# Queries, keys and the next input rows: loads moved to the GpSimd queue

## The chip, the core and the metric

The kernel runs on one NeuronCore of a Trainium2 chip. The metric is the device time of one launch in microseconds (us), taken as a median over runs. A profiled execution of the same program gives the trace from which every duration below is read.

## What is computed

Two independent heads are computed and their outputs laid side by side. Head A is a long convolution done through Fourier transforms. Head B is a recurrent attention over 64 segments of 32 rows, each preceded by 8 memory rows that the segment before has produced:

```python
for s in range(n_seg):
    xs = x[:, s * seg_len:(s + 1) * seg_len, :].copy()
    h = jnp.concatenate([mem, xs], axis=1)
    q = jnp.einsum('btd,dhe->bhte', h, Wq)
    k = jnp.einsum('btd,dhe->bhte', h, Wk)
    v = jnp.einsum('btd,dhe->bhte', h, Wv)
    scores = jnp.einsum('bhqe,bhke->bhqk', q, k) * scale
    scores = jnp.where(mask[None, None], scores, -1000000000.0)
    p = _softmax(scores, axis=-1)
    o = jnp.einsum('bhqk,bhke->bhqe', p, v)
    o = jnp.einsum('bhte,hed->btd', o, Wo)
    mem = o[:, :M, :].copy()
    outs.append(o[:, M:, :])
```

There are 32 heads of 128, a model width of 1024, and a segment needs the memory rows of the one before, so segments cannot run side by side.

## The kernel before

A first phase, some 390 us long, does head A and, beside it, the projections of the last 8 rows of every segment, which do not depend on the memory. Their queries and keys go to a DRAM tensor `QKBd` and their values to `VBd`.

Then comes the loop over the 64 segments (L948); one pass is called a turn here. A turn treats the 32 rows that are 8 memory rows and the segment's first 24. Heads are worked on in four groups of eight (`u0` to `u3`): `qk_part` (L787) multiplies the transposed rows `hT` with the group's query and key weights, `v_part` (L803) with the value weights of two groups, `tr_a` (L825) transposes, `scores` (L848) forms the masked scores, `softmax` (L870) turns them into probabilities `P`, `blocks` (L887) spreads these into `PB`, `pv` (L896) multiplies with the values, and `wo` (L911) with the output weights, all groups summing into one accumulator `Y`. `Y` is copied to `Y_sb`, its memory rows are transposed by `fill_mem` (L932) into the next `hT` at L936, and the next turn begins.

Not all weights fit on the chip. A turn streams 17 pairs of 512 KB from DRAM through a ring of 5 buffers (`wring`). `done` (L768) calls `place` (L686) when TensorE has used a pair, and `place` issues the next load on SyncE's queue at L691. The loads keep one fixed order: query and key pairs, value pairs, output pairs, as the turn uses them; in two places of a turn a ring buffer is filled from a copy parked in PSUM (L762, L763) instead.

Besides the ring a turn moves five small things. `load_h` (L701) fetches the next turn's input rows into the tile `H` (128 partitions of 512 bytes, 64 KB), on ScalarE's queue at L708; `h_rows` (L923) transposes `H` on TensorE at L927, between `pv(u3)` and `wo(u3)`. `load_b` (L834) fetches the segment's own queries and keys from `QKBd` into `qkb` (512 pieces of 256 bytes, 128 KB), on SyncE's queue at L836; the next turn reads it first in `tr_a(u0)` (a GpSimd copy, L830). GpSimd's queue itself issues the old rows' accumulator `OLd` (L909, 64 KB), four output stores (L1030, 12 KB each) and the values `VB` (`load_vb`, L846, 64 KB). `qkb` and `H` have one buffer each; `H` shares its buffer with the tile `qks` of L800.

The order of every queue is the order in which the program is written (`manual_schedule`, L43). So the place of a call in the loop decides what stands before and behind it on its engine. Each group's `softmax` begins with a GpSimd instruction that clears half of `P` (L873); `P` has one buffer, so the clearing waits until `blocks` of the group before has read it.

Before the loop, L943 and L944 call `load_vb(0)` and `load_b(0)`, in that order.

Of the kernel before, what the change touches and what calls it, by code (L numbers as in the profile page):

```python
# [21 lines left out]
def fused_kernel(ctx: ExitStack, tc, q, k, v, shift_k, ssm_k, ssm_D, outa, x, mem0, Wq, Wk, Wv, Wo, outb, n_seg):  # L22
# [11 lines left out]
    nc = tc.nc  # L34
    S, D = 2048, 1024
    NP = 34
# [14 lines left out]
    QKBd = dram.tile([4, 128, n_seg * 128], BF, name="QKBd")  # L51
# [61 lines left out]
    def res_half(key, n):  # L113
        if key not in res:
            if key in early:
                res[key] = wide["t"][:, early.index(key)]
            else:
                res[key] = res_pool[key].tile([128, 2, 1024], BF, name=f"W{key[0]}{key[1]}_{key[2]}")
        nc.sync.dma_start(res[key][:, n, :], half_src(key, n))
        return res[key][:, n, :]  # L120
# [580 lines left out]
    def load_h(s):  # L701

        H_ = acte.tile([128, 256], BF, tag="qks", name="H")
        if s == 0:
            nc.gpsimd.dma_start(H_[0:32, :], mem0.rearrange("t (dq c) -> (t dq) c", dq=4))
            nc.gpsimd.dma_start(H_[32:128, :], x[0:24].rearrange("t (dq c) -> (t dq) c", dq=4))
        else:
            nc.scalar.dma_start(H_[:], x[32 * s - 8:32 * s + 24].rearrange("t (dq c) -> (t dq) c", dq=4))  # L708
        return H_

    H = load_h(0)
# [47 lines left out]
    def unpark():  # L759
        while to_copy:  # L760
            key, t = to_copy.pop(0)
            nc.scalar.copy(t[:, 0, :], park[key][0][:])  # L762
            nc.vector.tensor_copy(t[:, 1, :], park[key][1][:])  # L763
# [23 lines left out]
    def qk_part(u, kcs):  # L787
        if kcs[0] == 0:
            u.qk = ps_a.tile([128, 512], F32, tag="a", name="qkacc")
        for kc in kcs:  # L790
            w = pair(("qk", u.g, kc))
            for t in range(2):
                for c2 in range(2):
                    p0 = 32 * (2 * t + c2)
                    nc.tensor.matmul(u.qk[p0:p0 + 32, :], lhsT=hT[:, kc, :], rhs=w[:, t, c2 * 512:(c2 + 1) * 512],  # L795
                                     start=(kc == 0), stop=(kc == 7), tile_position=(0, p0))
            done(("qk", u.g, kc))

    def qk_out(u):
        u.qks = acte.tile([128, 512], BF, tag="qks", name="qks")  # L800
        nc.scalar.copy(u.qks[:], u.qk[:])  # L801
# [31 lines left out]

    def load_b(s):  # L834
        qkb = acte.tile([128, 4, 128], BF, tag="qkb", name="qkb")
        nc.sync.dma_start(qkb[:], QKBd[:, :, s * 128:(s + 1) * 128].rearrange("g e x -> e g x"))  # L836
        return qkb

    def new_u(g):
        u = G()  # L840
        u.g = g
        u.qkb = qkb[:, g, :]
        return u
# [4 lines left out]
    def scores(u):  # L848
        S = ps_ts.tile([128, 4, 40], F32, tag="ts", name="S")
        qb = u.qkb.rearrange("e (h t r) -> e h t r", h=8, t=2)  # L850
        for c in range(4):
            nc.tensor.matmul(S[32 * c:32 * c + 32].rearrange("p a k -> p (a k)"), lhsT=ident[:, 32 * c:32 * c + 32],
                             rhs=mask[:].unsqueeze(2).to_broadcast([128, 2, 2, 40]), start=True, stop=False,
                             tile_position=(0, 32 * c))
        for i in range(2):
            for c in range(4):
                hh = 2 * c + i
                nc.tensor.matmul(S[32 * c:32 * c + 32, i, :], lhsT=u.QT[:, hh, :], rhs=u.KT[:, hh, :],
                                 start=False, stop=False, tile_position=(0, 32 * c))
        for i in range(2):  # L860
            for c in range(4):
                hh = 2 * c + i
                nc.tensor.matmul(S[32 * c:32 * c + 8, 2 + i, :], lhsT=qb[:, hh, 0, :], rhs=u.KT[:, hh, :],  # L863
                                 start=False, stop=(i == 1), tile_position=(0, 32 * c))
        mx = act.tile([128, 4], F32, tag="mx", name="mx")
        nc.vector.tensor_reduce(out=mx[:], in_=S[:], op=ALU.max, axis=AX.X)  # L866
        nc.vector.tensor_tensor(out=S[:], in0=S[:], in1=mx[:].unsqueeze(2).to_broadcast([128, 4, 40]), op=ALU.subtract)  # L867
        return S

    def softmax(u, S):  # L870
        P = act.tile([128, 2, 2, 2, 32], BF, tag="P", name="P")
        k0 = 8 * u.g
        nc.gpsimd.memset(P[:, 1], 0.0)  # L873
        Sv = S[:].rearrange("p (a i) k -> p i a k", a=2)
        nc.scalar.activation(P[:, 0], Sv[:, :, :, 0:32], ACT.Exp, scale=scale)  # L875
        nc.scalar.activation(P[:, 1, :, :, k0:k0 + 8], Sv[:, :, :, 32:40], ACT.Exp, scale=scale)  # L876
        sm = act.tile([128, 4], F32, tag="sm", name="sm")
        Pv = P[:].rearrange("p b i a k -> p b (i a) k")
        nc.vector.tensor_reduce(out=sm[:], in_=Pv.rearrange("p b x k -> p x b k"), op=ALU.add, axis=AX.XY)  # L879
        nc.vector.reciprocal(sm[:], sm[:])  # L880
        nc.vector.tensor_tensor(out=Pv, in0=Pv, in1=sm[:].unsqueeze(1).unsqueeze(3).to_broadcast([128, 2, 4, 32]),  # L881
                                op=ALU.mult)
        Pf = P[:].rearrange("p b i a k -> p (b i a k)")
        nc.vector.transpose(out=Pf, in_=Pf)
        u.PT = P[:].rearrange("p b i a q -> p (b i) (a q)")
# [58 lines left out]
    qkb = load_b(0)  # L944
# [3 lines left out]
    for s in range(n_seg):  # L948
        last = s + 1 == n_seg
        def first_loads(g):  # L950
            for key in (n_o[g - 1:g] if s == 0 and g else ()):
                for n in range(2):
                    res_half(key, n)

        first_loads(0)
        us = [new_u(g) for g in range(4)]
        u0, u1, u2, u3 = us
        qk_part(u0, range(0, 5))
        unpark()
        qk_part(u0, range(5, 8))  # L960
        qk_out(u0)
        v_part(0, range(0, 4))
        tr_a(u0)
        unpark()
        first_loads(1)
        qk_part(u1, range(0, 4))
        S = scores(u0)
        softmax(u0, S)
        if s == 0:
            nc.vector.memset(PB[:], 0.0)  # L970
        blocks(u0, "DDDD")
        qk_part(u1, range(4, 8))
        qk_out(u1)
        v_part(0, range(4, 8))
        tr_a(u1)
        u0.v = u1.v = v_out()
        first_loads(2)
        qk_part(u2, range(0, 4))
        S = scores(u1)
        softmax(u1, S)  # L980
        if last:
            spare = [key for key in resident if key[0] != "o" and key[1] < 1 + (key[0] == "qk") and key not in early]
            for key, at in zip([key for key in streamed if key[0] == "o"], spare):
                nc.sync.dma_start(res[at][:], Wst[key])
                res[key] = res[at]
            for s0, s1 in ((0, 32), (32, s)):
                nc.sync.dma_start(OLs[:, s0:s1].rearrange("e s h r -> e (s h r)"),
                                  OLd[:, s0:s1].rearrange("e s x -> e (s x)"))
        qk_part(u2, range(4, 8))
        qk_out(u2)  # L990
        pv(u0, s)
        blocks(u1, "DDDD")
        first_loads(3)
        qk_part(u3, range(0, 2))
        tr_a(u2)
        qk_part(u3, range(2, 6))
        S = scores(u2)
        softmax(u2, S)
        qk_part(u3, range(6, 8))
        qk_out(u3)  # L1000
        v_part(1, range(0, 1))
        pv(u1, s)
        blocks(u2, "DDDD")
        v_part(1, range(1, 2))
        tr_a(u3)
        v_part(1, range(2, 5))
        S = scores(u3)
        if not last:
            H = load_h(s + 1)
            qkb = load_b(s + 1)  # L1010
        softmax(u3, S)
        v_part(1, range(5, 8))
        u2.v = u3.v = v_out()
        Y = ps_a.tile([128, 512], F32, tag="a", name="yacc")
        wo(u0, Y)
        pv(u2, s)
        blocks(u3, "DDAA")
        wo(u1, Y)
        wo(u2, Y)
        pv(u3, s)  # L1020
        if not last:
            hT = new_hT()
            h_rows(H, hT, 8)
        wo(u3, Y)
        Y_sb = act.tile([128, 256], BF, tag="P", name="Y_sb")
        nc.scalar.copy(Y_sb[:], Y[:, 0:256])  # L1026
        if not last:
            fill_mem(hT, Y_sb)
        for dq in range(4):
            nc.gpsimd.dma_start(outb[32 * s:32 * s + 24, dq * 256:(dq + 1) * 256], Y_sb[32 * dq + 8:32 * dq + 32, :])  # L1030
        if not last:
            load_vb(s + 1)
# [88 lines left out]
```

## Time and profile before

| | |
|---|---|
| median of 3 runs | 2093.33 us (2092.27 to 2094.11) |
| the profiled execution | 2093.32 us |
| its span, first to last instruction | 2091.5 us |
| mean granted TensorE clock | 0.984 |
| TensorE busy | 1702.4 us, 81% |
| VectorE busy | 1115.3 us, 53% |
| ScalarE busy | 908.7 us, 43% |
| GpSimd busy | 413.1 us, 20% |
| moved by DMA | 728.64 MB, 348 GB/s |

The span is cut into the first phase (to about 388 us), the loop (to about 2018 us) and a last stage that multiplies the kept rows with the output weights. A queue that issues DMAs is named with a q behind its engine (SPq, ACTq); GpSimd's issues are listed as busy time of POOL. A DMA queue of its own belongs to each issuing engine: q1 is fed by SyncE, q10 by ScalarE, q0 by GpSimd. "To landing" runs from the start of the issue to the semaphore that tells of the arrival.

### The profile page before, as it was taken

How to read it: one execution, taken by the hardware profiler on the slowest of the kernel's cores; microseconds unless marked ns; L12 is line 12 of the kernel's file. 1: busy time of each engine (PE TensorE's matmuls, PEld its weight loads, DVE VectorE, ACT ScalarE, POOL GpSimd, SP SyncE). 2: the span in 40 equal slices, each digit the busy share in tenths (PEclk: the TensorE clock that was granted, in tenths of full speed). 3: DMA queues.
4: the chain of work that ended last, by engine and by line, in shares of the span. 5: the costliest groups of instructions: out<-in, count | busy, mean ns of one | idle time of the engine just before them, and what ended most of it. 6: DMA issues, size and time to landing. Idle time of an engine off the chain costs nothing. (4 is left out here: it accounts for less than half of the span.)

```text
span 2091.5 us, 73911 instructions
## 1 busy us (share of the span) xinstructions
PE 1702.4 (81%) x30484; PEld 894.2 (43%) x30514; DVE 1115.3 (53%) x3313; ACT 908.7 (43%) x2276; POOL 413.1 (20%) x1018
## 2 busy tenths in 40 slices
PE   5888987888788888888887878888888878888879
PEld 2433233444444444444444444444444444444449
DVE  6986833355555555555555555555555555555541
ACT  5556731244444444444444444444444444444430
POOL 2004730121111111111111111111212121111110
PEclk9999999999999999999999999999999999999999
DMA  6899989999999999999999999999999999999980
GB/s 236 282 346 362 343 287 381 352 377 372 356 375 368 365 360 370 372 366 375 358 368 353 367 358 372 359 377 358 371 358 378 363 352 351 374 370 379 368 337 23
DMA packets 266384, 728.64 MB, mean 348 GB/s; under 512 B 65007, under 2 KB 77183, under 8 KB 265277
## 3 DMA queue, kind: packets, MB, share of 16 engines
q1 hardware_dynamic: 239486, 686.65, 88.8%
q0 software_dynamic: 15520, 22.06, 3.3%
q10 hardware_dynamic: 11040, 15.21, 2.1%
q8 instruction: 239, 3.92, 0.7%
q14 instruction: 99, 0.81, 0.1%
HBM read 673.52 MB, written 56.56 MB: 349 GB/s over the span
## 5 line engine op out<-in xcount | busy, mean ns | idle before, releaser
L795 PE MATMUL qkacc<-Wqk,hT 128*32 128x512 bf16 x4096 | 338.5, 383 | 0.0
L795 PEld LDWEIGHTS <-hT 128*32 128x32 bf16 x8192 | 184.9, 96 | 236.3 <-issue 84.2
L916 PEld LDWEIGHTS <-OT 128*32 128x32 bf16 x8192 | 210.1, 96 | 109.5 <-issue 59.2
L795 PE MATMUL qkacc<-wring,hT 128*32 128x512 bf16 x2048 | 204.9, 389 | 31.3 <-DMA wring<-Wstqk 25.5
L763 DVE COPY wring<-park 128x1024 bf16<-128x1024 bf16 x128 | 88.6, 692 | 239.4 <-PE vacc L809 124.8
L875 ACT ACTIVATE P<-S 128x128 bf16<-128x128 f32 x256 | 71.1, 278 | 330.4 <-DVE S L867 244.3
L809 PE MATMUL vacc<-Wv,hT 128*32 128x512 bf16 x2560 | 209.8, 382 | 0.0
L809 PE MATMUL vacc<-wring,hT 128*32 128x512 bf16 x1536 | 154.7, 387 | 65.5 <-DMA wring<-in_B_Wv_dram 63.6
L809 PEld LDWEIGHTS <-hT 128*32 128x32 bf16 x4096 | 113.0, 95 | 184.4 <-issue 108.3
L762 ACT COPY wring<-park 128x1024 bf16<-128x1024 bf16 x128 | 130.7, 1021 | 138.9 <-PE qkacc L795 112.8
L894 DVE COPY PB<-P 32x160 bf16<-32x160 bf16 x896 | 172.9, 193 | 10.6
L879 DVE TENSOR_REDUCE sm<-P 128x4 f32<-128x256 bf16 x256 | 107.5, 420 | 128.6 <-ACT P L876 128.6
L831 ACT COPY QK<-tp 128x256 bf16<-128x256 bf16 x256 | 95.4, 373 | 185.7 <-PE tp L822 184.5
L795 PE MATMUL qkacc<-Wearly,hT 128*32 128x512 bf16 x2048 | 161.0, 391 | 18.4 <-DVE hT L936 17.9
L830 POOL COPY QK<-qkb 128x64 bf16<-128x64 bf16 x256 | 61.3, 239 | 564.5 <-PE tp L822 404.8
L916 PE MATMUL yacc<-wring,OT 128*32 128x256 bf16 x2520 | 126.7, 274 | 37.4 <-DMA wring<-Wsto 35.2
L905 ACT CAST OT<-otacc 128x256 bf16<-128x256 f32 x256 | 98.7, 386 | 130.4 <-PE otacc L901 130.4
L801 ACT CAST qks<-qkacc 128x512 bf16<-128x512 f32 x256 | 151.1, 590 | 4.2 <-PE qkacc L795 3.5
L1030 POOL DMA_DIRECT2D out_dram<-Y_sb x256 | 129.1, 511 | 84.8 <-ACT Y_sb L1026 82.8
L822 PE MATMUL tp<-ident,qks 128*128 128x128 bf16 x1024 | 102.4, 223 | 52.6 <-ACT qks L801 50.3
L866 DVE TENSOR_REDUCE mx<-S 128x4 f32<-128x160 f32 x256 | 83.2, 325 | 85.2 <-PE S L863 79.5
L901 PE MATMUL otacc<-PB,vsb 128*128 128x160 bf16 x512 | 97.6, 238 | 35.3 <-ACT vsb L816 35.3
(212 smaller groups left out, 2957.1 us busy)
## 6 DMA issues: line engine op xcount, KB each, us to landing
wring<-Wstqk SPq DMA_DIRECT2D x448, 512.0 KB, 6.2
wring<-in_B_Wv_dram SPq DMA_DIRECT2D x320, 512.0 KB, 6.7
wring<-Wsto SPq DMA_DIRECT2D x315, 512.0 KB, 6.3
SK<-s_sb SPq DMA_DIRECT2D x8, 1024.0 KB, 5.5
SU<-s_sb SPq DMA_DIRECT2D x8, 1024.0 KB, 8.9
QKBd<-stq ACTq DMA_DIRECT2D x4, 2048.0 KB, 9.5
Kg<-SK SPq DMA_DIRECT2D x16, 512.0 KB, 7.0
Ug<-SU SPq DMA_DIRECT2D x16, 512.0 KB, 8.3
```

What stands on the lines that cost most here:

```text
L762: nc.scalar.copy(t[:, 0, :], park[key][0][:])
L795: nc.tensor.matmul(u.qk[p0:p0 + 32, :], lhsT=hT[:, kc, :], rhs=w[:, t, c2 * 512:(c2 + 1) * 512], start=(kc == 0), stop=(kc == 7), tile_pos ...
L801: nc.scalar.copy(u.qks[:], u.qk[:])
L809: nc.tensor.matmul(vacc[0][32 * c:32 * c + 32, :].rearrange("p (n x) -> p n x", n=2), lhsT=hT[:, kc, :], rhs=w[:, :, c * 256:(c + 1) * 256 ...
L822: nc.tensor.transpose(tp[:, j * 128:(j + 1) * 128], src[:, j * 128:(j + 1) * 128], ident[:])
L831: nc.scalar.copy(u.QT.rearrange("e (c j) r -> e c j r", c=2), tv[:, 0])
L879: nc.vector.tensor_reduce(out=sm[:], in_=Pv.rearrange("p b x k -> p x b k"), op=ALU.add, axis=AX.XY)
L894: (nc.vector if by[c] == "D" else nc.gpsimd).tensor_copy(to, src)
L901: nc.tensor.matmul(o, lhsT=w[:, i * 128:(i + 1) * 128], rhs=PB[:, 2 * kb + i].rearrange("p c q -> p (c q)"), start=(kb == 0), stop=(kb == 1))
L905: nc.scalar.copy(u.OT[:].rearrange("e (c i) q -> e i c q", i=2), ov[:, :, :, 0:32])
L916: nc.tensor.matmul(Y[32 * dq:32 * dq + 32, 0:256], lhsT=u.OT[:, hh, 0:32], rhs=w[:, hh % 2, dq * 256:(dq + 1) * 256], start=(u.g == 0 and ...
L1030: nc.gpsimd.dma_start(outb[32 * s:32 * s + 24, dq * 256:(dq + 1) * 256], Y_sb[32 * dq + 8:32 * dq + 32, :])
```

## The change

`load_h` in the loop issues on GpSimd's queue in place of ScalarE's, `load_b` on GpSimd's in place of SyncE's, and the two calls stand behind `softmax(u3)` in place of before it.

```diff
         else:
-            nc.scalar.dma_start(H_[:], x[32 * s - 8:32 * s + 24].rearrange("t (dq c) -> (t dq) c", dq=4))
+            nc.gpsimd.dma_start(H_[:], x[32 * s - 8:32 * s + 24].rearrange("t (dq c) -> (t dq) c", dq=4))
...
         qkb = acte.tile([128, 4, 128], BF, tag="qkb", name="qkb")
-        nc.sync.dma_start(qkb[:], QKBd[:, :, s * 128:(s + 1) * 128].rearrange("g e x -> e g x"))
+        nc.gpsimd.dma_start(qkb[:], QKBd[:, :, s * 128:(s + 1) * 128].rearrange("g e x -> e g x"))
...
         S = scores(u3)
+        softmax(u3, S)
         if not last:
             H = load_h(s + 1)
             qkb = load_b(s + 1)
-        softmax(u3, S)
         v_part(1, range(5, 8))
```

`load_h` for the first segment was on GpSimd's queue already (L705, L706) and stays there.

## The prediction

> **What bounds the kernel now.** First the DMA view, cut to 500 to 1900 us so that only turns of the loop are in it. The digits are the busy share of the 16 DMA engines; under them stand packets, megabytes and share of each queue.
>
> ```profile
> DMA  9999999999999999999999999999999999999999
> DMA packets 181450, 511.70 MB, mean 365 GB/s; under 512 B 50841, under 2 KB 60473, under 8 KB 181188
> q1 hardware_dynamic: 162900, 494.64, 95.2%
> q0 software_dynamic: 10368, 9.76, 2.2%
> q10 hardware_dynamic: 7920, 3.61, 1.0%
> ```
>
> The shares add to 99.4% with the instruction queues: the loop runs at the speed of the DMA engines. To see what that time is made of I sorted the trace's packet records of 60 turns by queue and size, and divided their summed durations by 16. A turn (25.56 us from one L936 to the next) holds 23.59 us of 4096-byte ring packets (median 159 ns each), 0.59 us of `qkb` (512 packets of 256 bytes, 18 ns each), 0.24 us of `H` (128 of 512 bytes, 29 ns), 0.37 us of 4096-byte packets on q0 (median 159 ns) and 0.6 us of small things.
>
> Second, the waits in the same window, to see where TensorE feels it. Columns: total us, times, longest.
>
> ```profile
> PE vacc L809 <- DMA wring<-in_B_Wv_dram: 54.0, 102, 1.8
> PE yacc L916 <- DMA wring<-Wsto: 29.9, 59, 1.6
> PE qkacc L795 <- DMA wring<-Wstqk: 23.9, 40, 1.7
> ```
>
> TensorE waits for ring loads some 2 us in each of these 55 turns, half of it for the value weights just after a turn begins. An engine wait shorter than that is made up there; a saving of DMA time is not lost there.
>
> Third, the tile `H`: the idle time before its transposes, and its way from issue to landing.
>
> ```profile
>   DMA H<-in_B_x_dram: 25.0, 40
> DMA to landing us min/median/max: 4.0/4.9/6.6
> ```
>
> `H` is needed as soon as it lands in many turns, so a later `H` is felt at once. Fourth, the timeline of one turn's end, for the places of the issues.
>
> ```profile
> 1018.17 0.37 SPq L836 DMA_DIRECT2D qkb<-QKBd  x1
> 1018.23 0.35 ACTq L708 DMA_DIRECT2D H<-in_B_x_dram  x1
> ...
> 1018.52 0.20 POOL L873 MEMSET P<- 128x128 bf16 x1 [1.24 <-DVE PB L894]
> 1018.64 0.45 SPq L691 DMA_DIRECT2D wring<-Wsto  x1
> ...
> 1023.61 0.28 PE L927 MATMUL x_tp<-ident,H 128*128 128x128 bf16 x2 [0.80 <-DMA H<-in_B_x_dram]
> ...
> 1023.78 0.56 POOL L909 DMA_DIRECT2D OLd<-OL  x1 [5.06 <-DVE OL L907]
> ```
>
> GpSimd has 5 us free behind the clearing of `P`.
>
> **The change, part by part.** *Issue time.* SyncE loses 0.37 us, and its next ring issue, 0.45 us here where a median one is 0.33, gets shorter and about 0.5 us earlier. ScalarE loses 0.35 us inside an idle gap of 1.61 us before its exponential. GpSimd gains two issues: 0.56 us (the `VB` row, also 64 KB) and 0.76 us (the `VBd<-stv` row, also 512 pieces). They fit into the 5 us. All three I cost at nothing: the engines' DMA share is 1.01 in the 2 us around the issue, so an earlier ring load only queues, and without GpSimd's gap 1.3 us would fall on the `OLd` issue, which nobody awaits.
>
> *DMA time.* On q0 the trace shows whole packets where the hardware queues show single rows: `OLd`, 128 rows of 512 bytes, is 16 packets of 4096 bytes of 165 ns. `H` has the same shape, so 128 x 29 ns becomes 16 x 165 ns; over 16 engines 0.24 becomes 0.17 us, a gain of 0.07. For `qkb` no row has 256-byte pieces on q0. If they pack as well, 32 x 159 ns / 16 = 0.32 us, a gain of 0.27; if a piece keeps its 18 ns, no gain; a loss of the same 0.27 has no row that excludes it. I take 46 ns per KB, the rate of q0's smallest packets (1024 bytes of the output stores): 128 x 46 / 16 = 0.37, a gain of 0.22. A check: summed over 1 to 5 us behind the issue, the ring moves 0.37 MB less than at its 395 GB/s, 0.94 us of lost ring time (0.74 if 375 is the base), against 0.83 in the packet records; so these packets do take what they show. Together **-0.29 us a turn**; ends +0.20 and -0.45 (0.94 less 192 KB at 395 GB/s).
>
> [...]
>
> *A later H.* The issue moves behind the clearing of `P`: over the 63 turns the clearing ends 0.48 us after ScalarE's issue began. From issue to landing q10 took 4.97 us on average; on q0 `VB`, a load of the same size, 5.14, and `OLd`, issued by an idle GpSimd as `H` will be, 5.53, its first packet starting 3.2 us after the issue against 1.8 for `H`; the two `H` loads of the first segment on q0 took 4.9 and 5.8. So +0 to +0.9; I take +0.4, between `VB` and `OLd`. `H` lands **0.9 us later**. In the 55 turns with a recorded landing `H` lies ready 0.15 us on average before use, so its transposes come 0.75 later; `wo(u3)` behind them waits 0.23 us on average for its ring pair, which takes that up: taken turn by turn, `Y` ends 0.53 us later. Next stand the ring waits of the new turn's first products, up to the fourth pair of `v_part(0)`: 1.08 us on average, 0.71 at the 5th percentile. They swallow 0.53. The pairs waited for there were issued before `H` is used, so they do not slip. With the DMA gain of 0.3 shortening the same waits, the turn-by-turn count leaves a cost of **+0.06 us**.
>
> The two ring loads issued late (behind `wo(u3)`'s pair and the first query pair) land 6.5 and 5.9 us after issue, queued behind others; a ring load of the loop lands within 4.7 at its quickest tenth, so half a microsecond is covered there.
>
> *A wait at the start.* `load_b(0)` moves too. In GpSimd's queue it stands behind `load_vb(0)`:
>
> ```profile
> 388.01 0.75 POOL L191 DMA_DIRECT2D VBd<-stv  x1 [2.40 <-issue]
> 394.35 0.56 POOL L846 DMA_DIRECT2D VB<-VBd  x1 [5.59 <-DMA VBd<-stv]
> 394.90 0.25 POOL L830 COPY QK<-qkb 128x64 bf16<-128x64 bf16 x1
> ```
>
> `VB` waits until the values have landed in DRAM, so `qkb` is issued at 394.9 (before: 384.7) and lands 5.0 (`VB`) to 6.2 us (`VBd<-stv`) later, near 401. The copy L830 and the first scores, at 395.21 before, come 6 us later, and TensorE has nothing else, being in program order. Ring loads issued by 395 keep the DMA engines busy until about 399.5; the next is released by TensorE near 402. Between 4 and 6.5 us are lost; I take **+5 us, once**.
>
> *Sum*, on the profiled execution's 2093.32 us (0.01 under the median): 63 x (-0.29 + 0.06) = -14.5, +5.0: **2083.8 us**, 0.45% faster. Nothing outside loop and start changes.
>
> **The rivals.**
> *The packets get no cheaper.* Only `H` gains 0.07: the count leaves about -0.05 a turn, -3, and the start adds 5: 2095 us, within 0.2%. For it: no 256-byte row on q0. Against: 512-byte rows pack at full rate.
>
> *H becomes the bound.* GpSimd starts `H` from idle, and if landing takes 1 us more than on q10 (`OLd`'s worst tenth is 5.9 us, the lone row of 5.8 us), `H` is 1.5 us late. The waits behind it hold about 0.9 us of late `Y`, so it decides from 1.2 us of lateness: there a turn gains 0 to 0.1, at 1.5 it loses 0.10 to 0.19 where the packet gain is small or none. 63 x 0.15 = 9.4, and 5 at the start: 2108 us, slower. For it: `OLd`'s late first packet. Against: `VB` at 5.14.
>
> [...]
>
> *The DMA engines are not what ends a turn.* Then nothing but the start is seen: 2098 us, slower by 0.24%. Against: 99.4%.
>
> **How the numbers follow.** The forecast has 0.5, the cheap-packet failure 0.2, the late `H` 0.25, the last 0.05. About 0.2%, 4.2 us, is what a measurement tells from no change. Faster 0.5, same 0.2, slower 0.3. The forecast's own range is 2073 to 2089 (-0.45 + 0.06 a turn with 4 at the start; -0.15 with 5). To hold 8 in 10 it must reach into the late `H`: 2073 to 2107. The cheap end of the packet price is inside it; the dear one (+0.20 + 0.06 a turn: 2115) lies in the two tenths left out.
>
> **What would show it.** Right: in the loop's DMA view q10 gone, q0 with 48 more 4096-byte packets a turn, q1 less 512; the turn 0.2 us shorter; more wait for `H` at L927 in nearly all turns, less for value weights at L809; first scores near 401. Wrong: 256-byte packets on q0; `H` landing over 5.9 us; value waits gone while the turn is longer.

## The result and the profile after

The changed kernel takes **2117.75 us** (median of 10 runs, 2110.05 to 2124.8), the kernel before on the same chips 2098.72 us (10 runs): a ratio of **1.0089, 95% interval 1.0062 to 1.0117**, 18.7 us slower. The forecast was 2083.8 us. The profiled execution took 2122.26 us (span 2120.5); its granted clock is 0.973, before 0.984. The turn went from 25.56 to 25.86 us.

DMA view of the kernel after, 500 to 1900 us, with packets, megabytes and share of each queue:

```profile
DMA packets 147595, 506.97 MB, mean 362 GB/s; under 512 B 22532, under 2 KB 25124, under 8 KB 147336
q1 hardware_dynamic: 132577, 482.76, 92.8%
q0 software_dynamic: 14759, 20.56, 4.8%
```

q10 is gone, the small packets are less than half as many, and yet fewer bytes per second arrive. Sorted as in the prediction, the packet records of a turn hold 0.377 us of `qkb` (32 packets of 4096 bytes; before 0.589), 0.267 of `H` (16 packets; before 0.236) and 23.84 of ring packets (before 23.59). All queues together hold 25.46 us a turn, before 25.42: what the two loads save, the ring's packets, as many as before, take more.

The waits of the kernel after in the same window (total us, times, longest):

```profile
PE x_tp L927 <- DMA H<-in_B_x_dram: 59.2, 55, 4.5
PE vacc L809 <- DMA wring<-in_B_Wv_dram: 46.9, 83, 1.9
PE qkacc L795 <- DMA wring<-Wstqk: 19.5, 33, 1.6
PE yacc L916 <- DMA wring<-Wsto: 5.8, 17, 0.8
```

The line on `H` in the same view of the kernel before:

```profile
PE x_tp L927 <- DMA H<-in_B_x_dram: 10.3, 18, 1.8
```

TensorE now waits for `H` in all 55 turns. Its three ring waits shrank from 107.8 to 72.2 us, by 0.65 us a turn, but the `H` wait grew more, from 10.3 us to 59.2. The tile `H` of the kernel after, with the waits of the issuing engine among them:

```profile
  DMA H<-in_B_x_dram: 129.3, 110
  POOL P L873: 19.2, 52
...
DMA to landing us min/median/max: 4.4/5.0/5.9
```

The way from issue to landing is nearly that of before (median 4.9 us); the issue is late. The end of a turn, from GpSimd's timeline and TensorE's (start, duration, instruction, idle before and its releaser):

```profile
1033.12 0.20 POOL L873 MEMSET P<- 128x128 bf16 x1 [1.24 <-DVE PB L894]
1033.69 0.55 POOL L708 DMA_DIRECT2D H<-in_B_x_dram  x1 [0.37 <-POOL P L873]
1034.23 0.79 POOL L836 DMA_DIRECT2D qkb<-QKBd  x1
...
1039.18 0.29 PE L927 MATMUL x_tp<-ident,H 128*128 128x128 bf16 x2 [1.71 <-DMA H<-in_B_x_dram]
```

The issue does not follow the clearing at once: GpSimd idles 0.37 us in between. Counted from the end of `scores(u3)`, as means over the turns, in us before and after: issue of `H` 0.23 and 1.12 us, landing 5.21 and 6.22, its transposes 5.44 and 6.26, the next `hT` 8.19 and 8.44, first product with a value pair from the ring 10.93 and 11.23.

The start, GpSimd's timeline of the kernel after:

```profile
396.59 0.55 POOL L846 DMA_DIRECT2D VB<-VBd  x1 [5.42 <-DMA VBd<-stv]
397.13 0.77 POOL L836 DMA_DIRECT2D qkb<-QKBd  x1
403.51 0.24 POOL L830 COPY QK<-qkb 128x64 bf16<-128x64 bf16 x1 [5.61 <-issue]
```

`qkb` lands 6.2 us after its issue and the copy starts at once. From the first transposes of `H` to the first scores it takes 13.76 us, before 7.58: **6.2 us lost, once**.

**An account of TensorE's turn.** Every us of a turn is either TensorE busy or a wait that something ended; a ring wait is one that the landing of a `wring` load ended. The mean over 62 turns, in us, says where a profile's turn got longer. The matmuls are the same in all these kernels, so "busy" changes only with their speed:

| kernel (edits below) | turn | busy | wait for `H` | ring waits | other waits |
|---|---|---|---|---|---|
| before | 25.56 | 20.82 | 0.17 | 1.97 | 2.59 |
| after | 25.86 | 20.87 | 1.10 | 1.32 | 2.56 |
| after, a second profile | 26.00 | 21.06 | 1.20 | 1.31 | 2.43 |
| `no_start` | 25.82 | 20.89 | 1.02 | 1.45 | 2.46 |
| `qkb_only` | 25.52 | 20.81 | 0.34 | 1.78 | 2.59 |
| `h_only` | 26.15 | 21.24 | 1.24 | 1.06 | 2.61 |
| `h_late_act` | 27.54 | 21.93 | 2.10 | 1.05 | 2.46 |
| `h_early` | 25.53 | 20.70 | 0.63 | 1.62 | 2.58 |
| `h_early_act` | 25.73 | 20.96 | 0.20 | 1.95 | 2.61 |
| `calls_ahead` | 25.85 | 20.55 | 0.25 | 1.57 | 3.49 |

From before to after: `H` +0.93, ring -0.65, busy +0.05 (+0.24 in the second profile). One profile carries 0.1 to 0.2 us of chance: the two of the changed kernel differ by 0.15, and `start_only`, whose loop is that of before, shows a turn of 25.63. So the ratios decide, and this table says what they are made of.

### The profile page after: what moved, and what is told of

The parts are those of the page before. It is cut to its first block, busy times and chain, and to the rows that moved or that the text cites. A ratio compares the mean times of both kernels' runs of the same rounds, so it can differ in the third digit from the quotient of the medians.

```text
span 2120.5 us, 74002 instructions
## 1 busy us (share of the span) xinstructions
PE 1713.3 (81%) x30514; PEld 895.0 (42%) x30514; DVE 1119.0 (53%) x3313; ACT 910.9 (43%) x2276; POOL 497.3 (23%) x1145
## 5 line engine op out<-in xcount | busy, mean ns | idle before, releaser
L795 PE MATMUL qkacc<-Wearly,hT 128*32 128x512 bf16 x2048 | 171.7, 414 | 18.4 <-DVE hT L936 17.9
```

## The experiments

The theories. **A**: the later `H` makes TensorE late at the turn's end, and with it the following ring requests. **A'**: of these only one matters, the refill for the sixth value pair (5) of the next turn's first value group. **B**: packets on GpSimd's queue slow the ring, whenever they come. **C**: TensorE's clock falls to half (0.50 in the clock records, 3413 ns at the shortest) where it has waited too long at the turn's end, and this carries the loss. All ratios are against the kernel before on the same chip.

**One load at a time.** `h_only` (`H` alone, as in the change):

```diff
-            nc.scalar.dma_start(H_[:], ...)
+            nc.gpsimd.dma_start(H_[:], ...)
...
-            H = load_h(s + 1)
             qkb = load_b(s + 1)
         softmax(u3, S)
+        if not last:
+            H = load_h(s + 1)
```

> Only the load of H goes to GpSimd's queue, behind softmax(u3); qkb stays on SyncE's queue where it was. Theory A (a late H makes TensorE late at a turn's end, so the next value pair is asked for late): H is needed 0.8 us or more after pv(u3) has ended, as in the changed kernel, and the turn is 0.2 to 0.3 us longer: +12 to +19 us on the kernel before, no wait at the start. Theory B (packets of GpSimd's queue slow the ring, whatever their timing): H is a third of the bytes moved, so a third of the loss: +4 to +6 us. The prediction's sum: -0.07 + 0.06 us a turn, no change.

Measured: **1.0150** (1.0114 to 1.0185), 31 us slower: more than the whole change, and more than either theory named.

`qkb_only` (`qkb` alone; the first one stays on SyncE):

```diff
-        nc.sync.dma_start(qkb[:], ...)
+        (nc.sync if s == 0 else nc.gpsimd).dma_start(qkb[:], ...)
...
             H = load_h(s + 1)
-            qkb = load_b(s + 1)
         softmax(u3, S)
+        if not last:
+            qkb = load_b(s + 1)
```

> Only the load of qkb in the loop goes to GpSimd's queue, behind softmax(u3); H stays on ScalarE's queue where it was, and the first segment's qkb stays on SyncE's queue. Theory A: H is as early as before, so the packet gain of about 0.2 us a turn is seen: -6 to -13 us. Theory B: two thirds of the loss remain: +8 to +12 us. The prediction's sum: -0.22 us a turn, -14 us.

Measured: **0.9973** (0.9948 to 0.9998), 5.7 us faster. The account shows why it is not the 0.22 us a turn (14 us) of the prediction: the ring waits fell by 0.19, but `H` landed 5.53 us after the scores' end instead of 5.21 and TensorE waited 0.17 longer for it. Other profiles say the same: `qkb_only_q2` (below) shows 1.84 us of ring waits and 0.34 for `H`, and three whose `qkb` and `H` are issued in the loop as before (`start_only`, `before_q2`, `h_early_act`) show 1.95 to 2.13 and 0.13 to 0.20. B expects a loss here; it falls.

`no_start` (the change, but the first `qkb` stays on SyncE; against the changed kernel):

```diff
-        nc.gpsimd.dma_start(qkb[:], ...)
+        (nc.sync if s == 0 else nc.gpsimd).dma_start(qkb[:], ...)
```

> The changed kernel with the first segment's qkb left on SyncE's queue. Both theories: the first scores come near 396 us and not near 404, and the kernel is 5 to 7 us faster than the changed one, so +11 to +14 us on the kernel before. If the start is made up later: as the changed one, +19 us.

Measured: **1.0061** (1.0039 to 1.0084); the loop alone loses 13 us. Against `qkb_only` that is 0.88%, 18.5 us or 0.29 us a turn: what `H` costs on GpSimd's queue at this place when `qkb` has moved too. The two moves do not simply add: taken in the other order, `H` alone costs 31 us and `qkb` then wins 18. `H` lands at 6.20 us in `no_start` and at 6.45 in `h_only`, with 18 and 40 windows at half clock (below); why it lands later in `h_only` stays open.

`start_only` (the first `qkb` alone on GpSimd's queue):

```diff
-        nc.sync.dma_start(qkb[:], ...)
+        (nc.gpsimd if s == 0 else nc.sync).dma_start(qkb[:], ...)
```

> The kernel before with only the first segment's qkb on GpSimd's queue, behind load_vb(0). All theories: its first scores come 6 to 7 us later after the first transposes of H than before, and the whole is 4 to 7 us slower (0.2 to 0.33%). If the start is made up by full ring buffers: within 2 us.

Measured: **1.0048** (1.0022 to 1.0075). The first scores came 13.98 us after the first transposes of `H` (7.58 before): 6.4 us, inside the interval of 4.6 to 15.7 us (the ratio itself says 10).

**The lateness without the queue.** `h_late_act` (only the call of `load_h` moves behind `softmax(u3)`; `H` stays on ScalarE, where two exponentials of that softmax now stand ahead of it):

```diff
-            H = load_h(s + 1)
             qkb = load_b(s + 1)
         softmax(u3, S)
+        if not last:
+            H = load_h(s + 1)
```

> Nothing goes to GpSimd: only the call of load_h stands behind softmax(u3), so ScalarE issues it behind its two exponentials, some 1.4 us later than before. Theory A: H lands 1.3 us later or more, the wait before its transposes is over 1 us, and the turn is 0.3 to 0.5 us longer: +19 to +32 us. Theory B: no packet of GpSimd's queue is added, so no change (within 4 us). The prediction's sum, which let a late Y be swallowed up to 0.9 us: within 5 us.

Measured: **1.0552** (1.0513 to 1.0592), 116 us, with no packet moved to another queue; A had expected a quarter of it. `H` was issued at 1.35 us and landed at 7.47 (before 0.23 and 5.21), so half of its lateness is a longer way, 6.1 us in place of 5.0. DMA view of `h_late_act`, 500 to 1900 us:

```profile
DMA packets 167805, 474.61 MB, mean 339 GB/s; under 512 B 46709, under 2 KB 55557, under 8 KB 167563
...
q1 hardware_dynamic: 150571, 458.70, 90.6%
```

With the other queues the engines are busy 94% of a time in which they move 7% fewer bytes a second (339 against 365 GB/s). The ring's packets, the same in number and size, take 24.23 us of a turn where before they took 23.59, so their time is not a fixed price of the bytes. A busy share near the top is no proof that the bytes set the pace.

In the account of `h_late_act` half of the loss is not a wait: busy time grew by 1.11 us a turn. It is the clock: its mean is 0.930, before 0.984. Page of `h_late_act`, clock in 40 slices, tenths:

```profile
PEclk9999999998999999988999998989998899899999
```

and the windows view of the kernel after (PE, PEld, DVE, ACT, POOL busy, then clock, DMA share, GB/s) over one turn's end:

```profile
1704.90:1708.40 3.50, 2.86 (x95) 2.13 (x82) 2.74 (x11) 1.30 (x5) 1.54 (x3) 1.00 1.04 417
1708.40:1711.90 3.50, 1.45 (x44) 1.03 (x36) 0.47 (x3) 0.93 (x3) 0.55 (x1) 0.99 1.01 343
1711.90:1715.30 3.40, 2.61 (x36) 1.34 (x36) 0.53 (x2) 0.37 (x1) 0.37 (x1) 0.50 0.98 389
1715.30:1718.70 3.40, 3.33 (x32) 1.24 (x36) 0.71 (x2) 0.95 (x1) 2.20 (x5) 0.50 0.75 243
```

In the second row TensorE is busy 41% of the time (1.45 of 3.50 us); in the next two the clock is 0.50. In the clock records of all loops these drops lie on one fixed grid of 3413 ns, and TensorE's busy share in the grid window before tells whether one comes. In the kernel after, a full-clock window with a busy share under 0.53 was followed by half clock 13 times of 17, one from 0.53 to 0.56 once of 6, one above that 0 times of 427; in `h_late_act`, 52 of 55 under 0.50, 0 of 362 above 0.53; in `h_only`, 25 of 26 under 0.53, 3 of 8 up to 0.56, 0 of 399 above. So in these three kernels the edge is not sharp, and lies near 0.53. A half-clock window is followed by another where its own busy share is under 0.82 (all 17 of `h_only` and the kernel after), not above (0 of 42). Half-clock windows in the 62 turns: 9 before, 19 and 30 after, 40 in `h_only`, 81 in `h_late_act`, 11 in `qkb_only`.

In the kernel after, `no_start`, `h_only` and `h_late_act`, mean waits for `H` of 1.0 to 2.1 us a turn went with 18 to 81 half-clock windows.

**The lateness filled with work.** `late_warm` adds matmuls to `h_late_act` in the place where TensorE waits for `H`; they write columns of `Y` that nothing reads:

```diff
         if not last:
+            for _ in range(18):
+                nc.tensor.matmul(Y[:, 256:512], lhsT=ident[:], rhs=VB[:], start=False, stop=False, skip_group_check=True)
             hT = new_hT()
             h_rows(H, hT, 8)
```

> h_late_act with 18 added matmuls of 128x256 ahead of the transposes of H, into columns of Y's bank that nothing reads; they run while TensorE would wait for H. Theory C (most of h_late_act's loss is TensorE at half clock, granted because a 3.4 us window was busy for less than some 53%): the windows at half clock fall from some 53 to below 15, and of the 116 us lost two thirds come back: +25 to +50 us on the kernel before. Theory A alone (late refills, clock a by-product): H is as late as in h_late_act, +105 to +125 us.

Measured: **1.0337** (1.0306 to 1.0369). With more work per turn it is 46 us faster than `h_late_act`: 2 half-clock windows in place of 81. Less than C expected: 40% of the loss came back, not two thirds. That is the clock's part at the least, for the other 70 us hold, beside the lateness, the added matmuls as far as they outlast the wait.

`h_only_warm` (10 such matmuls in `h_only`):

> h_only with 10 added matmuls of 128x256 ahead of the transposes of H, into columns of Y's bank that nothing reads. Theory C (windows at half clock carry most of the loss): they fall from 40 to 10 or fewer, the turns fall from 26.2 us to 25.5 to 25.75, +5 to +15 us on the kernel before. Late refills alone: as h_only, +25 to +37 us.

Measured: **1.0058** (1.0035 to 1.0082) where `h_only` has 1.0150: 12 us lost in place of 31, with 6 half-clock windows in place of 40, so some 60% of that loss is the clock. The first products of a turn whose weights need no load show it; groups of instructions, 500 to 1900 us, of before, `h_only`, `h_only_warm` and `h_late_act` in that order (count, then busy us and mean ns):

```profile
L795 PE MATMUL qkacc<-Wearly,hT 128*32 128x512 bf16 x1728 | 136.6, 393 | 15.3 <-DVE hT L936 15.3
```

```profile
L795 PE MATMUL qkacc<-Wearly,hT 128*32 128x512 bf16 x1696 | 154.6, 447 | 15.0 <-DVE hT L936 15.0
```

```profile
L795 PE MATMUL qkacc<-Wearly,hT 128*32 128x512 bf16 x1732 | 132.8, 383 | 15.3 <-DVE hT L936 15.3
```

```profile
L795 PE MATMUL qkacc<-Wearly,hT 128*32 128x512 bf16 x1632 | 175.2, 518 | 14.5 <-DVE hT L936 14.5
```

The same instructions take 393, 447, 383 and 518 ns on average.

`nostart_warm` (9 such matmuls in `no_start`):

> no_start with 9 added matmuls of 128x256 ahead of the transposes of H, into columns of Y's bank that nothing reads. Theory C: the windows at half clock fall from 15 to 8 or fewer, and some 8 us of no_start's 13 come back: +2 to +8 us on the kernel before. Theory A alone (late refills): +11 to +15 us, as no_start. If the added work delays the transposes instead: over +15 us.

Measured: **1.0054** (1.0023 to 1.0086), with 7 half-clock windows where `no_start` has 18. It cannot be told from `no_start`'s 1.0061, and C's +2 to +8 us is missed (11 measured). For the change itself the clock's part is therefore not shown by a ratio; its account gives it 0.05 and 0.24 us a turn in two profiles.

**An earlier H.** `h_early` (`no_start` with `H` issued right behind `tr_a(u3)`; the order of the calls against before):

```diff
         tr_a(u3)
+        if not last:
+            H = load_h(s + 1)
         v_part(1, range(2, 5))
         S = scores(u3)
+        softmax(u3, S)
         if not last:
-            H = load_h(s + 1)
             qkb = load_b(s + 1)
-        softmax(u3, S)
```

> H and qkb on GpSimd's queue as in the changed kernel, but load_h is called right behind tr_a(u3), before the clearing, and the first segment's qkb stays on SyncE's queue. GpSimd can then issue H some 1.5 us earlier than in the changed kernel and 0.6 us earlier than ScalarE did. Theory A (the late H is the cause in the loop): the wait for H at its transposes is gone and the packet gain remains: -6 to -16 us on the kernel before. Theory B (the packets of GpSimd's queue slow the ring): as no_start, +12 us.

Measured: **0.9985** (0.9963 to 1.0008), 3 us faster and not to be told from no change. The issue did not come as early as meant. Tile `H` of `h_early`, and its issue in GpSimd's timeline:

```profile
  DMA H<-in_B_x_dram: 79.1, 93
  PE vacc L809: 75.4, 54
```

```profile
1013.52 0.56 POOL L708 DMA_DIRECT2D H<-in_B_x_dram  x1 [1.40 <-PE vacc L809]
```

GpSimd waits 1.4 us, in nearly all turns, until TensorE is done with `scores(u3)`; the view names the value product that runs right behind. In nine turns of ten the issue starts 657 to 659 ns after the scores' end, here as in `calls_ahead` (below), although the two programs call `load_h` on different sides of `scores`. (The tile `QK` of L828, which the scores read, has the buffer tag of `H`; that this sharing is the reason is argued, not tried.) On average the issue starts at 0.70 us, against 1.11 in `no_start` and 0.23 before, and `H` lands at 5.85 (6.20; 5.21). These 0.35 us turn +0.61% into -0.15%, with both loads on GpSimd's queue and the same packets. It is lateness, not the queue: B falls here too. Nor is every bit of lateness equally dear. Set beside `qkb_only`, where `H` lands at 5.53, the first 0.32 us cost 2.5 us in all, within the noise, and 0.67 us (`no_start`) cost 18.5.

`h_early_act` (`load_h` stays on ScalarE):

```diff
         tr_a(u3)
+        if not last:
+            H = load_h(s + 1)
         v_part(1, range(2, 5))
         S = scores(u3)
         if not last:
-            H = load_h(s + 1)
             qkb = load_b(s + 1)
```

> The kernel before, with load_h called right behind tr_a(u3): ScalarE issues H about 0.5 us earlier, qkb and all else as before. Theory A: the 0.17 us of waiting for H a turn goes, with fewer half-clock windows: -3 to -10 us. Theory B and a loop bound by DMA alone: no change (within 4 us).

Measured: 1.0020 (0.9992 to 1.0048), not to be told from no change. But the edit did not make the issue earlier. Timeline of `h_early_act`, the end of `scores(u3)` and the issue:

```profile
1004.96 0.23 PE L863 MATMUL S<-QK,qkb 128*8 128x40 bf16 x8
...
1005.41 0.35 ACTq L708 DMA_DIRECT2D H<-in_B_x_dram  x1
```

It starts 0.22 us after the scores, at the median the same 216 ns as before, wherever the call stands. So this run does not say what an earlier `H` would win, and the expected 0.5 us were not to be had by the place of the call.

`calls_ahead` (the queues of `no_start`, the calls left ahead of `softmax(u3)`):

```diff
-            nc.scalar.dma_start(H_[:], ...)
+            nc.gpsimd.dma_start(H_[:], ...)
...
-        nc.sync.dma_start(qkb[:], ...)
+        (nc.sync if s == 0 else nc.gpsimd).dma_start(qkb[:], ...)
```

> As no_start, but both calls stand ahead of softmax(u3), so GpSimd issues H and qkb and only then clears P. H is issued some 0.8 us earlier than in no_start and lands at most 0.5 us later than before; the clearing comes 1.3 us later, and the second exponential of u3 waits for it by up to 0.5 us. If H's lateness is the loss in the loop: -6 to +3 us on the kernel before. If the place of the calls does not matter: +10 to +15 us, as no_start.

Measured: **1.0059** (1.0037 to 1.0080), against the expectation, although the `H` wait is short (0.25 us) and only 7 windows are at half clock. Timeline of `calls_ahead`:

```profile
1007.59 0.57 POOL L708 DMA_DIRECT2D H<-in_B_x_dram  x1 [1.39 <-PE vacc L809]
1008.14 0.79 POOL L836 DMA_DIRECT2D qkb<-QKBd  x1
...
1008.90 0.24 POOL L873 MEMSET P<- 128x128 bf16 x1
...
1009.17 0.20 ACT L876 ACTIVATE P<-S 128x32 bf16<-128x32 f32 x1 [0.69 <-POOL P L873]
1009.27 0.58 ACT L816 CAST vsb<-vacc 128x512 bf16<-128x512 f32 x1
...
1009.90 0.24 PE L901 MATMUL otacc<-PB,vsb 128*128 128x160 bf16 x1 [1.45 <-ACT vsb L816]
```

The clearing now waits for two issues (0.57 and 0.79 us), the exponential for the clearing, the copy of the values for the exponential, and TensorE for the copy. From the waits of `calls_ahead`, 500 to 1900 us (before, the same line has 30.4 us in 53 turns):

```profile
PE otacc L901 <- ACT vsb L816: 82.0, 54, 4.0
```

It is the 0.9 us of "other waits" in the account. Here the issues of two DMAs on an engine that also computes cost what stands behind them.

**The one late refill.** `nostart_q2`, `before_q2` and `qkb_only_q2` are `no_start`, before and `qkb_only`, but take the first group's query and key pairs in another order, so that a ring buffer comes free earlier (the start flag of the sum goes to the pair that is now first):

```diff
-        qk_part(u0, range(0, 5))
+        qk_part(u0, (2, 0, 1, 3, 4))
```

> no_start with one order changed: qk_part(u0) starts with its third weight pair, (qk,0,2), so that its ring buffer is free, and the load of the value pair (v,0,5) is issued, some 0.4 us earlier after hT is ready. Theory A' (late TensorE costs a turn only through this one late refill; the wait for the first value pairs swallows the rest): (v,0,5) is issued and lands 0.2 to 0.4 us earlier, the turn is 0.15 to 0.3 us shorter than in no_start: -5 to +4 us on the kernel before. If the lateness costs on another way (the matmuls after hT themselves): as no_start, +11 to +15 us.

> The kernel before with the same order in qk_part(u0). Theory A' : if that refill sets the turn in the kernel before too, (v,0,5) lands earlier and the turn is 0.1 to 0.3 us shorter: -6 to -19 us. If the turn is set by the bytes moved: no change (within 4 us).

> qkb_only (measured 0.27% faster) with the same order in qk_part(u0): the version that the runs point to. Theory A': both add: -10 to -22 us on the kernel before. Bytes moved set the turn: as qkb_only, -2 to -10 us.

Measured: 1.0075 (1.0045 to 1.0104), 1.0013 (0.9983 to 1.0044) and 0.9971 (0.9943 to 0.9998). In `nostart_q2` the refill was asked for 0.33 us earlier than in `no_start` and landed 0.12 earlier; the time did not fall. (The intervals of the two leave room for a gain of some 5 us, not for the 9 to 19 that A' named.) A' finds no support, and `qkb_only_q2` is `qkb_only` again.

`after_again` (the changed kernel once more):

> The changed kernel once more, beside the others on one chip: +15 to +23 us, as measured before; by every theory.

Measured: 1.0096 (1.0058 to 1.0134).

## Why the prediction was wrong, point by point

*"The loop runs at the speed of the DMA engines."* The share of 99.4% does not show it: `h_late_act` is 94% busy at a 7% lower rate, and the ring's packets took 23.84 us a turn after and 24.23 in `h_late_act` for what took 23.59 before. Packet time that the two loads save need not come off the sum of all queues, and did not (25.42 and 25.46).

*DMA time, -0.29 us a turn.* Right in kind (the 256-byte pieces pack: 32 packets, 0.377 us where 0.37 was taken), too large in size: `H` got dearer by 0.03 instead of cheaper by 0.07, which makes -0.18. (In `h_only`, with no `qkb` behind it on q0, `H` takes 0.21, cheaper by 0.02.) The second half failed, "a saving of DMA time is not lost there": alone, `qkb` on GpSimd's queue shortened the ring waits by 0.19 us a turn and lengthened the wait for `H` by 0.17; 5.7 us were left. The time of `qkb`'s packets fell by 36% (0.589 to 0.377 us).

*A later H.* The lateness came out right, 0.9 us forecast and 1.01 measured, but by luck, for its two parts were wrong in opposite ways: the issue is 0.89 us later, not 0.48, since GpSimd idles 0.4 us behind the clearing, and the way to landing is 0.13 longer, not 0.4. The transposes came 0.82 us later (0.75 forecast).

*"They swallow 0.53", +0.06 us a turn.* **This is the step that failed most.** The ring waits did shrink, by 0.65 of the 0.93 us that the `H` wait grew; 0.28 stayed. The experiments price it at 0.29 us a turn (`no_start` against `qkb_only`), 18.5 us where the forecast had 4. Swallowing does happen, but its limit is lower than the 1.2 us of lateness that the prediction named: with `H` landing 0.64 us later than before (`h_early`) hardly anything is lost against `qkb_only`, with 0.99 (`no_start`) the 18.5 us. Two things were missing. The turn-by-turn count let each wait shrink by all that TensorE came late, as if the loads it waits for came at fixed times; arrival of the first value pairs did stay (10.87 and 12.35 us after the scores, 10.82 and 12.34 before), but later requests slipped, such as that of the sixth value pair by 0.31 us. That such slips carry the 0.28 is argued; A' tried the one refill and found nothing, and which request matters stays open. And a wait was taken as lost time only, while the clock of what followed also fell (40 half-clock windows in `h_only`, 9 before). In `h_only` this is the larger part (busy +0.42 us a turn, and the ring waits swallowed 0.91 of 1.07); in the change itself two profiles put it at 0.05 and 0.24, and no ratio shows it.

*A wait at the start, +5.* Right: 6.2 us in the trace.

*Issue time at nothing.* Right for this place: 0.55 and 0.79 us fit into GpSimd's gap. `calls_ahead` shows the price one instruction further up.

*Sum.* -14.5 + 5 forecast; measured -5.7 for `qkb` (by `qkb_only`), +18.5 for `H` (the rest of `no_start`) and +6.2 at the start (by the trace): +19.0, where the ratio of the whole says +18.7. The split between `qkb` and `H` holds for this order of the moves alone. By it, of some 28 us between forecast and result, 15 are the price of the late `H`, 13 the DMA saving (63 x -0.29 = -18.3 forecast) and 1 the start.

*The rivals.* "The packets get no cheaper" fell for `qkb` and held for `H`. "H becomes the bound" had the direction and nearly the size (14.7 us over its base, measured 18.7), but put its beginning at 1.2 us of lateness; 1.0 was enough, and the clock was no part of it. "The DMA engines are not what ends a turn" had 0.05 and was nearer to the truth than the forecast: the saving went into another wait. Named as signs of right and seen: q10 gone, 48 more packets on q0, fewer small ones on q1, more wait for `H`, less for the values. Of the signs of wrong, one half came true: the value waits fell by 13% while the turn grew. The shorter turn, a sign of right, did not come.

Fastest of all are `qkb_only` and `qkb_only_q2`, 0.27% and 0.29% below before, the intervals just clear of 1.

## What to carry to other kernels

Split the busy engine's loop time into busy time and waits by releaser, and ask of every saved transfer which wait comes up next; a DMA share of 99% does not answer that. A load on which a serial step depends goes on the queue that can issue it first, and if it must come later, try the lateness alone before trusting that other waits swallow it. Where TensorE's waits lie close together, count its busy share in windows of 3.4 us too: here, where that share lay under about 0.53, the clock of the next window mostly fell to 0.50 (13 times of 17 in the kernel after), and the kernels with 18 or more half-clock windows waited 1.0 to 2.1 us a turn for `H`, the kernel before 0.17.

## What was not expected of the hardware

A busy share under about 0.53 in one full-clock window of the 3413-ns grid was followed by half clock (13 times of 17 in the kernel after; one above 0.56 never, in 427), and one under 0.82 in a half-clock window by another (all 17 of `h_only` and the kernel after). GpSimd's issue of `H` behind its own clearing of `P` began 0.37 us after that had ended at the median, 0.42 on average. On q0 `H` took 16 packets of 4096 bytes whose mean is 267 ns at a median of 169; in `h_only` the mean is 212. At the median `H`'s issue starts 216 ns after the scores' end on ScalarE's queue (before, `h_early_act`) and 658 on GpSimd's (`h_early`, `calls_ahead`).
